# Transposing weight loads, a tanh gate and a new order of work in a fused attention and gate block

## The chip, the cores and the metric

The kernel runs on one core of a Trainium2 chip. The metric is device time in microseconds for one execution; lower is better. A core has five engines with instruction queues of their own: TensorE (PE, matrix products, with PEld for its weight loads), VectorE (DVE), ScalarE (ACT), GpSimd (POOL) and SyncE (SP), which here only issues DMAs. Sixteen DMA engines move the data.

## The reference

Two residual blocks over 2048 rows of 448 numbers in bf16. The first is linear attention with 16 heads of width 28 and learned feature maps, the second a gated layer with 1792 inner columns.

```python
x = A_x
h  = x + A(layernorm(x))
h2 = h + B(layernorm(h))

def A(x):                       # per head, width 28
    q, k, v = split(x @ wqkv)
    pq, pk = q @ w_phi[h], k @ w_phi[h]
    phi_q = concat(softmax(pq), softmax(-pq))
    phi_k = concat(softmax(pk), softmax(-pk))
    kv, z = phi_k.T @ v, phi_k.sum(rows)
    return (phi_q @ kv) / (phi_q @ z + 1e-6) @ wo   # heads side by side

def B(x):
    return (sigmoid(x @ w_gate) * (x @ w_up)) @ w_down
```

## The kernel before, in words

**Tiles.** The 2048 rows are 16 tiles of 128 rows (t = 0 to 15). The 448 columns are cut in four parts of 112 (KT) on the input side, in four groups of four heads (G) for features, and in seven parts of 64 (NJ) for the gated layer, where two products of 64 rows run side by side on TensorE. The gated layer works on chunks of 2, 4, 4, 4, 2 tiles (CH) with 14 blocks of 128 inner columns each.

**Fold.** `w_fold` (L547) multiplies the key weights, and then the query weights, by the feature weights ahead of time, so that one product gives pk or pq: wk and wq are loaded whole (L514, L517), transposed by TensorE in 32 small products (L555), evicted in eight copies (L562) to WkT and WqT, multiplied by a block-diagonal Wphi (L570) and evicted (L578) to Wk2 and Wq2.

**Key stage**, per tile: statistics (L590, L592, L593), the reciprocal root on GpSimd (L595), the normalised tile xn (L607 for tiles 0 and 1, else ScalarE at L612), its transpose xnT (TensorE and an eviction at L630 for the first NPE = 2 tiles, else one transposing DMA for two tiles, L633), the key product (kp, L648), two exponentials exp(pk) and exp(-pk) (L661, L663), their sums per head (ss, L672), reciprocals (rs, L675), the features phi = e/sum (L677, on GpSimd), the value product (vp, L656) with its eviction v1 (L669; by VectorE for tiles 3, 7, 11, 15, else ScalarE), and the product kv of features and values, gathered in two PSUM banks over all tiles (L686).

**Query products** (q, L704) come in groups g by chunks c of 512 rows: 16 groups, each followed by two exponentials eq (L715). Groups with c >= QLATE = 3 wait for the last key product.

**Ramp.** After the last kv: kvz (L722), per tile the numerators and denominators for both signs (num, L743), their eviction ocp (L749), a chain on VectorE (rSm, rr, b, c, rd, o; L760 to L774), the transpose oT (TensorE for tiles 0 and 1, else a transposing DMA, L794), the output projection wo_ (L801, L803), the residual sum h (L809), statistics (L812 to L817), hn and its transpose hT (L833 or L845).

**Gated layer**: per chunk and block, gate and up products (gu, L882 and L884), a sigmoid (sig, L891, ScalarE, to bf16), its product with up (hh, L899, VectorE), and per tile the down product (dn, L908; in halves for the last chunk, L918), the last sum (fin, L929) and the store (st, L932). Exponential and sigmoid are in different tables of ScalarE; `sigld` (L730) loads the sigmoid's table, after all eq, and every sigmoid waits for it. The first inner buffer hh0 lies on the memory of wqkv_sb, so the first hh wait for all query products and the last value product.

**Order.** `_Graph.task` takes each piece of work with its engine, an assumed duration and its dependences. `order` plays the program through with these durations: whenever an engine is free it takes the ready task that can start first, and among equals the one of the highest priority. The priorities are written out by hand in `PLACE` (a list of numbers for each kind of task; a lower number goes first). `emit` writes each engine's queue in that order, with semaphore waits; nothing is reordered on the chip. All DMAs but one go out from SP's one queue: x in six loads, the weights, the transposes, the stores. The late weights (wo, gate, up, down: `late`) wait for named xn tiles, wd for kvz. `trw` (L526) is a transpose of the identity whose result is not used. `plan_warm` puts products of the identity (L462) into TensorE's gaps.

Of the kernel before, what the change touches and what calls it, by code (L numbers as in the profile page):

```python
# [5 lines left out]
dt = mybir.dt  # L6
# [4 lines left out]
P = 128  # L11
D = 448
# [87 lines left out]
    "gu": """-149 -69 212 504 -67 499 571 613 553 686 662 556 704 811 760 897 430 682 831 777 916 981 800 922  # L100
        1060 933 899 1065 980 1044 1074 1055 1069 1091 1426 1071 1096 1414 1351 1802 1426 1463 1803 1796
        1792 1803 1804 1805 1841 1845 1857 1849 1914 1897 1891 1901 1973 1977 1913 1978 2489 2015 2513 2543
        2509 2613 2613 2544 2690 2667""",
    "sig": """948 372 885 604 191 749 554 125 566 -25 401 65 70 404 1365 1163 1121 1732 1149 1516 1414 1417 837
        1305 1745 568 1524 1733 1778 1672 1896 1696 2258 1698 1277 1813 1360 1866 1312 1490 1487 1911 1594
        2084 1373 1485 2455 1646 1813 1209 2197 1782 1347 2343 1785 1546 2315 2249 923 2294 1937 2190 2255
        1783 1989 1863 1460 2849 2249 2072""",
    "hh": """-350 -346 71 178 -275 119 344 313 177 836 837 195 770 762 1030 1300 355 1247 1023 1310 1073 1339
        1341 1165 1768 1355 1139 1150 1428 1144 1128 1619 1849 1209 1161 1615 1564 1460 1637 1568 1864 1791
        1386 1144 1440 1563 1682 1730 1603 1465 2178 1685 1693 1665 1679 1142 1889 2077 2002 1895 1899 2065  # L110
        1937 1755 2251 1517 1783 1620 1747 1911""",
# [15 lines left out]
class _Graph:  # L127
# [38 lines left out]
    def order(self):  # L166
# [55 lines left out]
        while True:  # L222
            best = None
            for e in self.ENGINES:
                cands = []
                for t in ready[e]:
                    est = max(free[e], port) if t.lock else free[e]
                    if e == "pe" and t.rows64 != rows64:
                        est += self.SWITCH
# [30 lines left out]
            elif t.kind == "tr":  # L260
                t.finish = max(t.finish, dma_free + 1.0)
# [720 lines left out]
```

## Time and profile before

| | us |
|---|---|
| median of 3 runs | 219.78 |
| lowest, highest | 219.76, 220.05 |
| profiled execution, its own time | 221.35 |
| span of that execution, first to last instruction | 219.6 |
| TensorE busy | 206.8 (94%) |
| VectorE busy | 133.4 (61%) |
| ScalarE busy | 116.5 (53%) |
| GpSimd busy | 52.5 (24%) |

Times in rows of the profile count from the start of the span. A matmul's busy time contains its way through the array, so that matmuls in a row overlap; what a run of them takes is read from the chain of waits, where "PE bank L648 x4" stands with the time until the next piece. L numbers are lines of the kernel before.

### The profile page before, as it was taken

The numbers are of one execution on the slowest core, as the hardware profiler recorded it, in microseconds if no ns is written. First come the engines' busy times: TensorE is split into PE (matmuls) and PEld (weight loads), VectorE is DVE, ScalarE is ACT, GpSimd is POOL, SyncE is SP. The second block draws the span as 40 slices with busy tenths as digits, with TensorE's granted clock in tenths as the row PEclk, the third lists the DMA queues.
The fourth block names the chain that finished last, engine by engine and source line by source line (L and its number), as shares of the span: only waits on it lengthen the run. The fifth ranks groups of instructions, "written<-read, shape, count | busy, mean of one in ns | idle before, by whom it ended". The sixth has DMA issues, their size and how long they took to land.

```text
span 219.6 us, 4860 instructions
## 1 busy us (share of the span) xinstructions
PE 206.8 (94%) x1912; PEld 119.3 (54%) x1912; DVE 133.4 (61%) x315; ACT 116.5 (53%) x203; POOL 52.5 (24%) x91
## 2 busy tenths in 40 slices
PE   6699997879999899999999999999999999999994
PEld 1665654546654577754444444445444455556893
DVE  2689878676299999996759754342344523224532
ACT  2689997975899748857554764220244321001420
POOL 5332898787101105072033300000000000000000
PEclk9889999999999999999999999999999999999999
DMA  6985999990282204566544740001000000111001
GB/s 173 277 165 94 199 179 201 198 154 3 63 226 48 43 3 72 98 128 149 109 41 84 87 84 1 3 8 56 23 0 3 0 3 32 51 42 44 1 3 42
DMA packets 37702, 17.51 MB, mean 80 GB/s; under 512 B 28912, under 2 KB 36784, under 8 KB 37680
## 3 DMA queue, kind: packets, MB, share of 16 engines
q1 hardware_dynamic: 37216, 17.19, 39.1%
q8 instruction: 15, 0.25, 0.4%
q10 hardware_dynamic: 464, 0.03, 0.1%
q14 instruction: 7, 0.06, 0.1%
HBM read 8.68 MB, written 1.84 MB: 48 GB/s over the span
## 4 chain that ended last, share of the span: by engine, by line
PE 67%; ACT 12%; DMA 10%; DVE 6%; issue 2%; SPq 1%; POOL 0%
PE bank L882 36%; PE bank L908 17%; DMA xnT<-xn_pad 6%; PE bank L801 4%; ACT eq L715 3%; DMA wqkv_sb<-in_A_wqkv_dram 3%; ACT xn_pad L612 2%; PE bank L918 2%; ACT ek L661 2%; PE bank L704 2%; ACT opm L749 2%; PE bank L656 2%; ACT v L669 1%; ACT ek L663 1%; DMA oT<-o_pad 1%
## 5 line engine op out<-in xcount | busy, mean ns | idle before, releaser
L882 PE MATMUL bank<-hnT,wgu_sb 64*128 64x512 bf16 (+1 forms) x490 | 87.2, 333 | 0.5 <-DVE st L812 0.3
L884 PE MATMUL bank<-hnT,wgu_sb 64*128 64x512 bf16 (+1 forms) x490 | 87.2, 334 | 0.0
L891 ACT ACTIVATE sg_sb<-bank 128x512 bf16<-128x512 f32 (+1 forms) x70 | 35.6, 510 | 74.8 <-PE bank L884 69.4
L882 PEld LDWEIGHTS bank<-hnT,wgu_sb 64*128 64x128 bf16 x490 | 45.4, 94 | 38.5 <-issue 1.2
L899 DVE TENSOR_TENSOR hh<-sg_sb,bank 128x512 bf16<-128x512 bf16 (+1 forms) x70 | 40.4, 579 | 40.3 <-ACT sg_sb L891 37.9
L884 PEld LDWEIGHTS bank<-hnT,wgu_sb 64*128 64x128 bf16 x490 | 45.3, 94 | 0.0
L908 PE MATMUL bank<-wd_sb,hh 128*128 128x448 bf16 x196 | 37.6, 353 | 0.2 <-DVE hh L899 0.2
L908 PEld LDWEIGHTS bank<-wd_sb,hh 128*128 128x128 bf16 x196 | 18.9, 98 | 18.7 <-issue 0.8
L677 POOL TENSOR_TENSOR phi<-ek,rsum 128x896 bf16<-128x896 bf16 x16 | 27.0, 1697 | 8.7 <-DVE rs L593 4.2
L929 DVE TENSOR_TENSOR x_sb<-bank,x_sb 128x448 bf16<-128x448 f32 (+1 forms) x18 | 10.2, 572 | 22.7 <-PE bank L908 19.0
L817 POOL TENSOR_TENSOR rs<-rs,neghalf 128x1 f32<-128x1 f32 x16 | 10.1, 634 | 53.0 <-DVE rs L815 52.9
L672 DVE TENSOR_REDUCE ssum<-ek 128x32 f32<-128x896 bf16 x16 | 17.1, 1070 | 7.4 <-ACT ek L663 5.9
L715 ACT ACTIVATE eq<-bank 112x512 bf16<-112x512 f32 x32 | 18.6, 647 | 1.9 <-PE bank L704 1.9
L841 ACT ACTIVATE hn_pad<-x_sb,nm,rs 128x896 bf16<-128x896 bf16 x14 | 15.8, 1129 | 3.6 <-POOL nm L839 2.3
L648 PE MATMUL bank<-Wk,xnT 112*128 112x448 bf16 x64 | 14.6, 353 | 3.3 <-DMA xnT<-xn_pad 3.3
L749 ACT CAST opm<-bank 128x960 bf16<-128x960 f32 x16 | 15.2, 968 | 2.9 <-PE bank L743 2.3
L704 PE MATMUL bank<-xnT,Wq 112*112 112x512 bf16 x64 | 16.4, 381 | 0.1
L656 PE MATMUL bank<-wqkv_sb,xnT 112*128 112x448 bf16 x64 | 15.1, 360 | 0.0
L590 DVE BATCH_NORM_STATS2 st<-x_sb 128x6 f32<-128x448 bf16 x16 | 9.7, 615 | 5.8 <-DMA x_sb<-in_A_x_dram 5.8
L801 PE MATMUL bank<-wo_sb,oT 64*128 64x448 bf16 x56 | 11.9, 349 | 0.4 <-DMA oT<-o_pad 0.3
L803 PE MATMUL bank<-wo_sb,oT 64*128 64x448 bf16 x56 | 11.9, 350 | 0.0
L612 ACT ACTIVATE xn_pad<-x_sb,nm,rs 128x448 bf16<-128x448 bf16 x14 | 10.4, 802 | 1.6 <-DMA xnT<-xn_pad 1.6
(80 smaller groups left out, 217.5 us busy)
## 6 DMA issues: line engine op xcount, KB each, us to landing
wgu_sb<-in_B_w_gate_dram SPq DMA_DIRECT2D x7, 224.0 KB, 6.0
wgu_sb<-in_B_w_up_dram SPq DMA_DIRECT2D x7, 224.0 KB, 5.8
wd_sb<-in_B_w_down_dram SPq DMA_DIRECT2D x7, 224.0 KB, 5.5
out_dram<-x_sb SPq DMA_DIRECT2D x14, 112.0 KB, 1.7
x_sb<-in_A_x_dram SPq DMA_DIRECT2D x3, 448.0 KB, 7.1
wqkv_sb<-in_A_wqkv_dram SPq DMA_DIRECT2D x3, 392.0 KB, 6.2
wo_sb<-in_A_wo_dram SPq DMA_DIRECT2D x8, 98.0 KB, 4.8
x_sb<-in_A_x_dram SPq DMA_DIRECT2D x1, 224.0 KB, 3.3
```

The source lines that it names most:

```text
L656: r = e.matmul(bank[b][:, 0:D], lhsT=xT(t, kt), rhs=wqkv_sb[:, kt, 2 * D:3 * D], start=(kt == 0), stop=(kt == KT - 1))
L672: task(("ss", t), "dve", 1.0, lambda e, s=s: e.tensor_reduce(ssum[:, s, :], ek[:, s, :, :].rearrange("p a (h d) -> p (a h) d", d=DH), AX.X ...
L677: task(("phi", t), "pool", 1.66, lambda e, t=t, s=s: e.tensor_tensor(phi[:, t % NPHI, :, :].rearrange("p a (h d) -> p (a h) d", d=DH), ek[ ...
L704: r = e.matmul(bank[b][:GP, :], lhsT=Wq2[:, kt, g * GP:(g + 1) * GP], rhs=xnT[:GP, 2 * c:2 * c + 2, :, kt, :], start=(kt == 0), stop=(kt = ...
L715: task((key, g, c), "act", 0.48, lambda e, g=g, c=c, sg=sg, nm=nm: e.activation(eq[c][:, sg, g, :], bank[got(nm)[0]][:GP, :], ACT.Exp, sca ...
L749: task(("ocp", t), "act", 0.845, lambda e, t=t: e.copy(opm[:, (t // 2) % 2, :, t % 2, :, :].rearrange("p b e h -> p b (e h)"), pair[got((" ...
L801: e.matmul(bank[b[0]][:, 0:D], lhsT=oT[0:64, tb, j, :], rhs=wo_sb[0:64, j, :], start=(j == 0), stop=(j == NJ - 1))
L882: e.matmul(bank[bg][:, 0:N], lhsT=wgu_sb[0:64, j, fs], rhs=hnT[0:64, j, cs], start=(j == 0), stop=(j == NJ - 1))
L884: r = e.matmul(bank[bu][:, 0:N], lhsT=wgu_sb[64:P, j, fs], rhs=hnT[64:P, j, cs], start=(j == 0), stop=(j == NJ - 1), tile_position=(64, 0))
L891: task(("sig", f_, c), "act", 0.487 if n == 4 else 0.27, lambda e, j=j, N=N, nm=nm: e.activation(sg_sb[:, j % NSG, 0:N], bank[got(nm)[0]][ ...
L899: task(("hh", f_, c), "dve", 0.605 if n == 4 else 0.34, lambda e, j=j, N=N, nm=nm, f_=f_, c=c: e.tensor_tensor(hhT[c % 2][:, f_, 0:N], sg_ ...
L908: r = e.matmul(bank[b][:, 0:D], lhsT=hhT[c % 2][:, f_, ts], rhs=wd_sb[:, f_, :], start=(f_ == 0), stop=(f_ == FT - 1))
```

## The change

- **Query and key weights.** wk and wq are not loaded. One transposing DMA each (`wT`, on SP) reads 512 columns of the weights from DRAM straight into WkT and WqT, in four blocks of 128 columns by 448. Blocks of 128 don't end where heads of 28 do, so Wphi gets two forms with blocks of six heads, zeros outside (masks maskW, two more products on GpSimd, four small loads from ScalarE's queue), and a fold takes up to two products per block. Only the value weights are loaded plainly (wv_sb). `trw` goes.
- **Gate.** sigmoid(g) = (tanh(g/2) + 1)/2: ScalarE writes tanh with scale 0.5 in f32, VectorE does (t + 1) * up in one operation, and the last sum multiplies by 0.5. `sigld` and the waits on it go; hh0 lies on wv_sb, Wk2, ek and phi, and the first hh wait for the last kv.
- **Late weights** wait for no tile; each gets a place in time in `PLACE`, before which `order` doesn't issue it.
- **Engines.** phi for tiles 5, 10 and 15 on VectorE; all v1 on ScalarE; tiles 2 and 3 transposed by TensorE too (NPE 4).
- **Query products** of chunks 1 to 3 wait for the last key product (QLATE 1), and the query fold uses banks 6 and 7 only.
- **Planner.** DMAs are assumed with other durations; all priorities in `PLACE` are new numbers.

```diff
-    "wk": """-54""",
-    "wq": """-31""",
-    "x": """-49 97 -66 153 194 403""",
-    "wv": """162""",
+    "x": """-1482 -1481 -1420 -108 80 110""",
+    "wv": """20""",
+    "wT": """-449 -50""",
-    "wo": """-284 -237 -109 -270 210 -133 380 376""",
-    "wg": """-425 -159 279 392 352 243 416""",
-    "wu": """-92 -32 -21 632 225 32 510""",
-    "wd": """306 59 205 -189 414 -101 56""",
+    "wo": """371 117 227 433 467 476 394 505""",
+    "wg": """505 491 155 372 315 471 206""",
+    "wu": """198 348 590 208 258 610 602""",
+    "wd": """385 721 711 677 665 660 781""",
...
+                    if t.kind == "in" and t.prio is not None:
+                        est = max(est, -0.1 * t.prio)
...
-            if t.kind == "in":
-                dma_free = max(dma_free, est + 1.5) + t.size / 300.0
-                t.finish = dma_free + 1.0
-            elif t.kind == "tr":
-                t.finish = max(t.finish, dma_free + 1.0)
+            if t.kind is not None:
+                dma_free = max(dma_free, est + 1.2) + t.size
+                t.finish = dma_free + t.full
...
-    NPE = 2
+    NPE = 4
-    QLATE = 3
+    QLATE = 1
-    V_DVE = (3, 7, 11, 15)
+    V_DVE = ()
+    PHI_DVE = (5, 10, 15)
...
-        sg_sb = sb("sg_sb", [P, NSG, 512])
+        sg_sb = sb("sg_sb", [P, NSG, 512], dt.float32)
...
+            task(("Wphi", w), "pool", 1.35, lambda e, w=w: e.tensor_tensor(
+                Wphi[:, w, :, :, :], Wphi0[:, w, :, None, :].to_broadcast([P, 4, 6, DH]),
+                maskW[:, w, :, :, None].to_broadcast([P, 4, 6, DH]), ALU.mult),
+                [("wphi", w, 0), ("wphi", w, 1), ("mphi0", w), ("mk2", w)])
...
-                    for kt in range(KT):
-                        r = e.transpose(bank16[b][:GP, kt * GP:(kt + 1) * GP],
-                                        wqkv_sb[:, kt, w * D + g * GP:w * D + (g + 1) * GP], ident[:GP, :GP])
+            WT, W2, c0, h0 = (WqT, Wq2, 0, 0) if w == 0 else (WkT, Wk2, D - 64, -2)
+            task(("wT", w), "sp", 1.3, lambda e: e.dma_start_transpose(out=WT[:, :, :], in_=A_wqkv[:, c0:c0 + 512]),
+                 lat=-0.4, size=2.1, kind="tr")
...
-                    for g in range(G):
-                        r = e.matmul(bank[b][:GP, g * GP:(g + 1) * GP], lhsT=WT[:, g, kt * GP:(kt + 1) * GP],
-                                     rhs=Wphi[:, g, :], start=True, stop=True)
+                    old = 0
+                    for k in range(4):
+                        base = 4 * k + h0
+                        hi = min(base + 6, H)
+                        for lo, z in ((max(base, 0), old), (old, hi)):
+                            if lo < z:
+                                r = e.matmul(bank[b][:GP, lo * DH:z * DH], lhsT=WT[:, k, kt * GP:(kt + 1) * GP],
+                                             rhs=Wphi[:, w, k, lo - base:z - base, :], start=(k == 0), stop=(k == 3 and z == hi))
+                        old = hi
...
-            task(("phi", t), "pool", 1.66, lambda e, t=t, s=s: e.tensor_tensor(
+            task(("phi", t), "dve" if t in PHI_DVE else "pool", 1.0 if t in PHI_DVE else 1.66, lambda e, t=t, s=s: e.tensor_tensor(
...
-        task("sigld", "act", 1.4, lambda e: e.activation(junk[:, 0:1], neghalf[:, 0:1], ACT.Sigmoid),
-             EQ_ALL + ["neghalf"])
...
-                    sg_sb[:, j % NSG, 0:N], bank[got(nm)[0]][:, 0:N], ACT.Sigmoid),
+                    sg_sb[:, j % NSG, 0:N], bank[got(nm)[0]][:, 0:N], ACT.Tanh, scale=0.5),
...
-                    hhT[c % 2][:, f_, 0:N], sg_sb[:, j % NSG, 0:N], bank[got(nm)[1]][:, 0:N], ALU.mult), deps, bias=bias)
+                    hhT[c % 2][:, f_, 0:N], sg_sb[:, j % NSG, 0:N], 1.0, bank[got(nm)[1]][:, 0:N], op0=ALU.add, op1=ALU.mult),
...
-                        xo, bank[got(nm)[0]][:, 0:w], xo, ALU.add),
+                        xo, bank[got(nm)[0]][:, 0:w], 0.5, xo, op0=ALU.mult, op1=ALU.add),
```

In the lists of late weights the numbers are tenths of a microsecond of the planner's time; in the list of x the first four loads go as soon as SP is free, by rank.

More of the change, by code (lines that the diff above doesn't have):

```diff
@@ L413, in build @@
         xnT = sb("xnT", [P, NT // 2, 2, KT, P])
-        wqkv_sb = sb("wqkv_sb", [GP, KT, 3 * D])
         Wq2 = sb("Wq2", [GP, KT, D])
-        Wk2 = sb("Wk2", [GP, KT, D])
-        Wphi0 = sb("Wphi0", [GP, G, DH])
-        Wphi = sb("Wphi", [GP, G, GP])
+        Wphi0 = sb("Wphi0", [P, 2, 4, DH])
+        maskW = sb("maskW", [P, 2, 4, 6])
+        Wphi = sb("Wphi", [P, 2, 4, 6, DH])
         wo_sb = sb("wo_sb", [P, NJ, D])
@@ L521, in build @@
         load_x(12, 16, bias=BIG - 8, dur=1.0)
-        load("wphi", Wphi0[:], A_w_phi.rearrange("(g hl) i j -> (hl i) g j", hl=HL), 25, bias=BIG, eng="act")
-        task("Wphi", "pool", 1.0, lambda e: e.tensor_tensor(
-            Wphi[:].rearrange("p g (h d) -> p g h d", h=HL), Wphi0[:][:, :, None, :].to_broadcast([GP, G, HL, DH]),
-            maskK[:][:, None, :, None].to_broadcast([GP, G, HL, DH]), ALU.mult), ["wphi", "maskK"])
-        task("trw", "sp", 1.25, lambda e: e.dma_start_transpose(out=oT[:, 0, 0, :], in_=ident[:]), ["ident"],
-             lat=2.8, kind="tr")
+        phi_rows = A_w_phi.rearrange("h i j -> (h i) j")
+        for w in range(2):
+            c0, one, z = (-64, slice(64, P), slice(0, 64)) if w else (0, slice(0, 64), slice(64, P))
+            full, part = (slice(1, 4), 0) if w else (slice(0, 3), 3)
+            task(("mphi0", w), "dve", 0.08, lambda e, w=w, z=z, part=part: e.memset(Wphi0[z, w, part, :], 0.0))
+            r0 = 64 if w else 0
+            load(("wphi", w, 0), Wphi0[:, w, full, :], phi_rows[r0:r0 + 384].rearrange("(b p) j -> p b j", p=P), 0.15,
+                 bias=BIG + w, eng="act")
+            r1 = 0 if w else 384
+            load(("wphi", w, 1), Wphi0[one, w, part, :], phi_rows[r1:r1 + 64], 0.1, bias=BIG + w, eng="act")
+            off = 8 if w else 0
+            task(("mk0", w), "pool", 0.15, lambda e, w=w: e.memset(maskW[:, w, :, :], 1.0))
+            task(("mk1", w), "pool", 0.2, lambda e, w=w, off=off: e.affine_select(
+                out=maskW[:, w, :, :], in_=maskW[:, w, :, :], compare_op=ALU.is_ge, fill=0.0, base=-off,
+                channel_multiplier=1, pattern=[[16, 4], [-DH, 6]]), [("mk0", w)])
+            task(("mk2", w), "pool", 0.2, lambda e, w=w, off=off: e.affine_select(
+                out=maskW[:, w, :, :], in_=maskW[:, w, :, :], compare_op=ALU.is_ge, fill=0.0, base=DH - 1 + off,
+                channel_multiplier=-1, pattern=[[-16, 4], [DH, 6]]), [("mk1", w)])
+            task(("Wphi", w), "pool", 1.35, lambda e, w=w: e.tensor_tensor(
+                Wphi[:, w, :, :, :], Wphi0[:, w, :, None, :].to_broadcast([P, 4, 6, DH]),
+                maskW[:, w, :, :, None].to_broadcast([P, 4, 6, DH]), ALU.mult),
+                [("wphi", w, 0), ("wphi", w, 1), ("mphi0", w), ("mk2", w)])
         late = []
@@ L655, in f @@
                 for kt in range(KT):
-                    r = e.matmul(bank[b][:, 0:D], lhsT=xT(t, kt), rhs=wqkv_sb[:, kt, 2 * D:3 * D],
+                    r = e.matmul(bank[b][:, 0:D], lhsT=xT(t, kt), rhs=wv_sb[:, kt, :],
                                  start=(kt == 0), stop=(kt == KT - 1))
@@ L692, in build @@
                  banks=[((4, 5), None)] if t == 0 else None, until=[("kvz", 0), ("kvz", 1)])
-        for name, dst, src, kb, dur, deps in late:
-            load(name, dst, src, kb, deps=deps, dur=dur)
+        for name, dst, src, took, dur, place in late:
+            load(name, dst, src, took, dur=dur, lat=0.65)
+            K.tasks[name].prio = -10 * place
         for c in range(NCH):
@@ L716, in build @@
                         eq[c][:, sg, g, :], bank[got(nm)[0]][:GP, :], ACT.Exp, scale=1.0 if sg == 0 else -1.0), [nm])
-        EQ_ALL = [(k, g, c) for k in ("eqp", "eqm") for g in range(G) for c in range(NCH)]
-        Q_ALL = [("q", g, c) for g in range(G) for c in range(NCH)]
         for sg in range(2):
```

121 lines of the change are left out of this document (55 added, 66 removed), and 130 rows, old and new, of the table PLACE.

## The prediction

> **What bounds the kernel now.** I read the page's span, slices and chain shares first, then the busy time by stretches, and then the chain of waits piece by piece.
>
> ```profile
> span 219.6 us, 4860 instructions
> PE   6699997879999899999999999999999999999994
> DMA  6985999990282204566544740001000000111001
> PE bank L882 36%; PE bank L908 17%; DMA xnT<-xn_pad 6%; PE bank L801 4%; ACT eq L715 3%; DMA wqkv_sb<-in_A_wqkv_dram 3%; ACT xn_pad L612 2%; PE bank L918 2%; ACT ek L661 2%; PE bank L704 2%; ACT opm L749 2%; PE bank L656 2%; ACT v L669 1%; ACT ek L663 1%; DMA oT<-o_pad 1%
> ```
>
> TensorE carries the end, but 10% of the chain is DMA: the loads of the query and key weights and the transposes of the normalised input. By stretches (span, PE, PEld, DVE, ACT, POOL busy, clock, DMA share, GB/s):
>
> ```profile
> 4.00:57.40 53.40, 48.00 (x372) 29.94 (x370) 40.64 (x95) 42.82 (x86) 34.79 (x33) 0.97 0.84 160
> 31.20:50.00 18.80, 15.51 (x127) 9.62 (x126) 13.43 (x20) 14.99 (x33) 15.23 (x12) 1.00 1.09 173
> 57.40:75.60 18.20, 16.42 (x173) 9.85 (x171) 15.84 (x48) 16.60 (x27) 1.49 (x2) 1.00 0.45 115
> 75.60:95.00 19.40, 18.80 (x282) 14.24 (x283) 18.84 (x55) 13.42 (x23) 4.43 (x12) 1.00 0.34 61
> 95.00:215.00 120.00, 120.00 (x1073) 63.31 (x1072) 56.63 (x117) 42.34 (x69) 9.72 (x30) 1.00 0.21 42
> ```
>
> From 95 to 215 us TensorE never rests, while VectorE and ScalarE work less than half the time. So the end can move only if TensorE gets its earlier work done sooner. That earlier work has two parts: the **key stage** (to the last feature product, L686) and the **ramp** (from there to about 95). Three engines are over 70% busy in 31 to 50 and the DMA engines are full (1.09). The chain of waits shows the ends of the parts:
>
> ```profile
> 2.40 6.20 DMA wqkv_sb<-in_A_wqkv_dram
> 9.46 0.53 PE bank L570 x8
> 14.54 0.54 ACT ek L663
> 31.24 6.89 DMA xnT<-xn_pad
> 42.19 6.79 DMA xnT<-xn_pad
> 49.03 0.93 PE bank L648 x4
> 50.38 0.76 PE bank L648 x4
> 56.40 0.42 PE bank L686 x8
> 56.81 0.88 PE bank L704 x4
> 75.63 0.27 PE bank L882
> ```
>
> The first key exponential is at 14.5, the key stage ends at 56.8, the first gate product is at 75.6. Two transposes (31.2 and 42.2) lie on the chain for 6.9 and 6.8 us. Against them stand the medians from issue to landing, and what SP had issued just before the second one:
>
> ```profile
> wqkv_sb<-in_A_wqkv_dram SPq DMA_DIRECT2D x3, 392.0 KB, 6.2
> x_sb<-in_A_x_dram SPq DMA_DIRECT2D x1, 224.0 KB, 3.3
> hnT<-hn_pad SPq DMA_TRANSPOSE x14, 2.9
> xnT<-xn_pad SPq DMA_TRANSPOSE x7, 6.3
> oT<-ident SPq DMA_TRANSPOSE x1, 7.9
> ```
> ```profile
> 0.79 0.46 SPq L503 DMA_DIRECT2D x_sb<-in_A_x_dram  x1
> 39.45 1.52 SPq L503 DMA_DIRECT2D wgu_sb<-in_B_w_gate_dram  x2
> 41.02 0.60 SPq L503 DMA_DIRECT2D wgu_sb<-in_B_w_up_dram  x1
> 42.19 1.23 SPq L633 DMA_TRANSPOSE xnT<-xn_pad  x1
> ```
>
> In a quiet queue a transpose lands in 2.9 us; behind three 224 KB loads it takes 6.8, so the late weights cost about 4 us at each of these two places.
>
> **The change part by part.**
>
> *Start.* The weights wk and wq no longer come as plain loads followed by 32 TensorE transposes and eight evictions (L555, L562); two transposing loads write WkT and WqT. In the new order SP issues x 0, x 1, x 2-3, WkT, so the WkT issue begins near 0.79 + 3 x 0.5 = 2.3. No row shows a transpose that reads DRAM. Its landing lies between 2.9 us (quiet) and 7.9 (oT<-ident, in the full queue of the start). I take 5.0, nearer the first end, since only 448 KB are queued ahead of it: 7.3. Four folds (L570, 0.53 us for eight matmuls, two folds in the old form; three eighths more columns in the new one) and an eviction of 0.6 (L578, quoted below) bring about 9.4, one key product (0.93 with its drain) 10.3, against 14.5: 4.2 us earlier, bounds 1.3 and 6.3. Value weights now come after both transposing loads, near 13, as late as before; no exponential waits for them, and the value product of a tile is wanted only with its features.
>
> The Trainium skill ("DMA: Bandwidth & Descriptors", Why small descriptors are slow) speaks against this part: DRAM reads in 256-byte pieces lose about 3 cycles in 11. The same page (Latency and other measured facts) gives a transpose 261 GB/s, by which, as an estimate, 459 KB take 1.8 us; no run here shows either. By these figures WkT lands nearer 6 than 7.3 and the sum improves by about 1 us.
>
> *Key stage.* VectorE gets three feature products (896 elements each), loses four value evictions and the four W copies; GpSimd loses three products; ScalarE gets the four value evictions and two more input evictions.
>
> ```profile
> L677 POOL TENSOR_TENSOR phi<-ek,rsum 128x896 bf16<-128x896 bf16 x16 | 27.0, 1697 | 8.7 <-DVE rs L593 4.2
> L672 DVE TENSOR_REDUCE ssum<-ek 128x32 f32<-128x896 bf16 x16 | 17.1, 1070 | 7.4 <-ACT ek L663 5.9
> L669 DVE CAST v<-bank 128x448 bf16<-128x448 f32 x4 | 2.4, 609 | 0.6 <-PE bank L656 0.4 <-PE bank L686 0.2
> L562 DVE COPY WqT<-bank 112x448 bf16<-112x448 bf16 x2 | 0.8, 377 | 0.0
> L578 DVE CAST Wk<-bank 112x448 bf16<-112x448 f32 x2 | 1.2, 602 | 0.0
> L590 DVE BATCH_NORM_STATS2 st<-x_sb 128x6 f32<-128x448 bf16 x16 | 9.7, 615 | 5.8 <-DMA x_sb<-in_A_x_dram 5.8
> ```
>
> A feature product on VectorE is not in the trace: between 1.07 (the sum over the same 896 elements) and 1.70 (on GpSimd); I take 1.07, since it is the same engine and length. VectorE then has 40.6 + 3 x 1.07 - 2.4 - 1.5 = 39.9 us from 4.1 on. GpSimd has 34.8 - 5.1 = 29.7 plus about 3 for the second Wphi and its masks. ScalarE loses twelve exponentials (next part), about 6.3, and gains six evictions of at most 0.6: 40.1 or less, and part of that overlaps. So VectorE paces the stage, with ScalarE close behind. Never idle, it ends at 44, and the last kv near 45; idle 12.8 us as now, at 56.8. Of the present idle time 5.8 is the wait for x (L590), which stays, and 7.4 the wait of L672 on the exponentials, mostly behind the late transposes, which goes where their queue is clear. I take 6 us idle: 50.0, and 50.3 with the last kv. **Term 1: -6.5**, bounds 0 and -11.8.
>
> *Query products.* With QLATE 1 the products of chunks 1 to 3 wait for the last key product.
>
> ```profile
> L704 PE MATMUL bank<-xnT,Wq 112*112 112x512 bf16 x26 | 6.8, 381 | 0.1
> L884 PE MATMUL bank<-hnT,wgu_sb 64*128 64x256 bf16 x98 | 12.0, 270 | 0.0
> L743 PE MATMUL bank<-kvz,eq 112*128 112x120 bf16 x120 | 8.7, 217 | 0.9 <-ACT opm L749 0.9
> L801 PE MATMUL bank<-wo_sb,oT 64*128 64x448 bf16 x35 | 7.4, 350 | 0.4 <-DMA oT<-o_pad 0.3
> 63.10 2.11 ACT L715 ACTIVATE eq<-bank 112x512 bf16<-112x512 f32 x4
> ```
>
> These are counts in 57.4 to 95. Some 26 matmuls (six groups of four) of the query product run there now; after it will be twelve, so six groups of 0.86 us (5.2 on TensorE) and twelve exponentials of 0.53 (6.3 on ScalarE) move behind the last key product. That product ends some 5 us ahead of the last kv (the key product at 50.4 to 51.1 against 56.8), and there TensorE has room: two groups fit, 1.7 us. **Term 2: +3.5**, bounds +1.7 and +5.2.
>
> *Ramp.* TensorE's own work in 57.4 to 95, by spacings: query 6.5 x 0.87 = 5.6; numerators 15 x 0.42 = 6.3; output projection 5 x 7 x 0.19 = 6.7; gate and up 98 x 0.109 = 10.7 (256 against 448 columns at 0.19); small transposes about 2: 31 of 37.6 us, a **gap** of 6. The added query work can lie in it, as nothing in the gate chain of tiles 0 to 5 waits for chunks 2 and 3, and no sigmoid waits for all exponentials. Against it, ScalarE is busy 16.6 of 18.2 at the ramp's front, where a table load goes:
>
> ```profile
> L730 ACT ACT_TABLE_LOAD x1 | 1.3, 1283 | 0.0
> ```
>
> I take half the gap. **Term 3: -3.0**, bounds 0 and -6.
> The weights for the down projection now go out between oT and hT transposes instead of in one run at 58; behind a load these land up to 4 us later (6.9 against 2.9), but the same query work covers TensorE there: nothing, with 4 us if it isn't there. The gate and up weights lose their waits on xn and stand at written places up to 61 us in SP's one queue, each behind the transposes ahead of it; issued by 61 and landed within 6.2 (the 392 KB row) they are there at 67, ahead of a first gate product that comes 18.8 us after the last kv (75.6 less 56.8), at 69. Later places would cost their whole lateness.
>
> *Gate.* tanh with scale 0.5 into f32, (t + 1) times u in one VectorE operation, the half in the last sum: as many instructions, elements and PSUM operands as before. Behind 120 us of unbroken TensorE they cost nothing; doubled, VectorE's 56.6 us would still fit. Only the five last gates of a chunk and the last sum are bare: 0, bounds -0.5 and +1.
>
> **Sum**: -6.5 + 3.5 - 3.0 = -6.0 on the span of 219.6, thus 213.6. The profiled execution took 221.35, 1.75 more than its span; the median of the runs, 219.78, lies 0.2 above the span, so the forecast for the runs is **213.8**.
>
> **The rivals.**
> 1. *The stage packs.* Transposes land in 3 us throughout, VectorE idles 3 us less, and two thirds of the gap fill: -9.5 + 3.5 - 4 = -10: 209.8. For it: the 7.4 us of waits on exponentials. Against: four engines with 30 to 40 us each leave little slack.
> 2. *The queue wins.* The start's DMA is full (slices at 8 to 9), and the transposing loads put off x 8-15 and wv; keys begin 1.3 earlier only. Stage -3: -3 + 3.5 - 3 = -2.5: 217.3.
> 3. *Slower: the query products lose their cover.* If VectorE idles as it does now, the stage ends near 55.3 (-1.5) with TensorE idle where six query groups lay; all 5.2 come behind it, and ScalarE, full at the ramp's front, holds up the numerators, so that only 1 us of the gap fills: -1.5 + 5.2 - 1 = +2.7: 222.5. It decides when the stage ends later than 56.8 - 4.2 = 52.6.
> 4. *Not one table.* If tanh and exp took turns in the tables, each turn costs 1.28; eight turns in the ramp, 10 us on an engine with 1.6 spare there: about +2 over all, 222. The trace shows a single load for exp, identity and copy together, and none for tanh. The Trainium skill ("ScalarE: Activation LUTs", Table sets) puts exp and tanh in one set; by that this rival falls.
>
> **How the numbers follow.** Forecast 0.50, packed stage 0.16, queue 0.14, lost cover 0.14, tables 0.03; 0.03 falls between the last three, within 0.2% of before (0.44 us, about what these runs can tell from no change). So faster 0.80, same 0.03, slower 0.17. The range reaches from below the packed stage to just over no change, 208.0 to 220.5, and leaves out the slower cases; the forecast's own range is 211 to 217.
>
> **What would show it.** First ek near 10.3 (before 14.5); last L686 near 50 (56.8); xnT landings with a median near 3 to 4 (6.3); VectorE busy 38 to 41 to the stage's end; query products after the last key product, TensorE without gaps over 1 us from 60 on; one table load; 95 to the end unchanged in length per product. A WkT landing after 10, a last kv after 52.6, or loads between exp and tanh would prove it wrong.

## The result, and the profile after

The changed kernel takes 214.73 us (median of 4 runs, 213.96 to 214.87) against 219.8 for the kernel before (median of 4, 219.76 to 220.05). The ratio is 0.976, 95% interval 0.9735 to 0.9784: 5.1 us faster, where 6.0 was forecast and 213.8 named. Line numbers below are those of the changed kernel, where L578 is the fold, L629 the transpose of a normalised tile on TensorE, L656 is the key product, L664 the value product, L694 the product kv, L685 the features, L713 the query product, L807 the output projection, L890 and L892 gate and up, L915 the down product.

The page of the changed kernel, the lines that answer to those shown of before:

```profile
span 212.9 us, 4844 instructions
PE   6799999999998998999999999999999999999994
DMA  6975773991037357564315610001000001111001
PE bank L890 38%; PE bank L915 18%; PE bank L807 4%; PE bank L713 4%; PE bank L656 3%; PE bank L664 3%; ACT eq L724 3%; DMA WkT<-in_A_wqkv_dram 2%; PE bank L925 2%; DMA oT<-o_pad 2%; ACT xn_pad L620 2%; PE bank L694 2%; ACT opm L753 2%; PE bank L578 1%; PE bank L747 1%
```

The input transposes are gone from the chain, DMA's share falls from 10% to 4%, and TensorE's slices are at 8 or 9 tenths from the third one on until the last. By stretches (columns as before), cut at the new ends of the parts:

```profile
4.00:49.80 45.80, 44.40 (x366) 27.98 (x365) 38.92 (x88) 41.22 (x85) 31.41 (x32) 1.00 0.81 175
49.80:68.60 18.80, 17.85 (x180) 11.11 (x178) 15.75 (x46) 17.09 (x29) 1.50 (x2) 1.00 0.30 64
68.60:95.00 26.40, 25.27 (x327) 17.50 (x329) 24.30 (x73) 16.47 (x27) 7.68 (x23) 1.00 0.57 127
```

The chain of waits shows where the parts end now, and one new wait:

```profile
2.18 5.13 DMA WkT<-in_A_wqkv_dram
7.36 0.93 PE bank L578 x14
8.29 0.23 PE bank L629 x4
8.51 0.37 PE bank L578 x7
8.91 1.22 DVE Wk L586 x2
10.27 0.92 PE bank L656 x4
48.96 0.84 PE bank L694 x16
68.73 0.27 PE bank L890
80.39 4.39 DMA oT<-o_pad
88.02 5.47 PE bank L915 x28
```

The key weights land at 7.3. The first exponential (11.22 in the timeline) comes 3.3 us earlier than in before's profile, the key stage ends at 49.8 instead of 56.8, the first gate product comes at 68.7 instead of 75.6, and the first down product at 88.0 instead of 94.6. So the whole gain is there at the end of the key stage: 3.3 us of it come before the first exponential, 3.7 between there and the last kv (38.6 us for 42.3). The ramp (last kv to first down product) takes 38.2 us, before 37.8. Two kinds of transposes and the transposing load of the key weights, median from issue to landing:

```profile
hnT<-hn_pad SPq DMA_TRANSPOSE x14, 2.6
xnT<-xn_pad SPq DMA_TRANSPOSE x6, 3.1
WkT<-in_A_wqkv_dram SPq DMA_TRANSPOSE x1, 5.1
```

The input transposes took 6.3 before. VectorE's wait for x, 5.8 before, has shrunk too:

```profile
L598 DVE BATCH_NORM_STATS2 st<-x_sb 128x6 f32<-128x448 bf16 x16 | 9.4, 611 | 2.7 <-DMA x_sb<-in_A_x_dram 2.7
```

The gate operations keep their durations, 595 ns for ScalarE and 685 for VectorE, against the 595 and 686 ns of before in the view by line and shape:

```profile
L905 DVE SCALAR_TENSOR_TENSOR hh<-sg_sb,bank 128x512 bf16<-128x512 f32 x42 | 28.6, 685 | 31.5 <-ACT sg_sb L899 31.3
L899 ACT ACTIVATE sg_sb<-bank 128x512 f32<-128x512 f32 x42 | 24.8, 595 | 43.7 <-PE bank L892 41.3 <-DVE hh L905 1.5 <-DVE mv L820 0.9
```

**Two different gains.** The spans of the two profiles differ by 6.7 us, the medians of the runs by 5.1. Both profiled executions end some 1.75 us after their spans (221.35 on 219.6; 214.7 on 212.9), so the median run of before has a span of about 218.0: before's profiled execution was 1.6 us longer than its median run. The four runs of before beside the result lie close together, but in the three jobs of the experiments its medians were 220.6, 221.0 and 221.2, near the profiled execution. `gate_sigmoid` below, whose median is that of the changed kernel (214.7), was 6.0 us faster than before in its own job. So the 5.1 holds for the four runs of the result, and the kernel before varies by more than the difference between 5.1 and 6.7. Its stretches at the start show one thing that varies (last three columns: the clock that TensorE was granted, as a share of the full one, DMA share, GB/s):

```profile
5.00:10.00 5.00, 2.94 (x39) 2.43 (x39) 3.14 (x15) 2.60 (x5) 1.46 (x3) 0.96 1.09 279
10.00:15.00 5.00, 4.95 (x39) 3.57 (x39) 5.00 (x17) 4.07 (x10) 1.14 (x2) 0.70 1.13 235
```

TensorE was busy 2.94 of 5 us while it waited for weights, and from 9.6 to 13.0 ran at half clock (0.70 over 5 us is 3 us at half), just when fold and first products were due. The Trainium skill ("TensorE: Matmul & The Clock Gate", Part 1) has the clock halve after an idle window of about 3.4 us. This trace shows no such window: between its first product and 9.6 TensorE's longest pause was 1.66 us (6.98 to 8.64), and in the 3.4 us ahead of 9.6 it was busy for 1.75.

### The profile page after: what moved, and what is told of

It is laid out like the page before. It is cut to its first block, busy times and chain, and to the rows that moved or that the text cites. A ratio compares the mean times of both kernels' runs of the same rounds, so it can differ in the third digit from the quotient of the medians.

```text
span 212.9 us, 4844 instructions
## 1 busy us (share of the span) xinstructions
PE 204.5 (96%) x1914; PEld 118.3 (56%) x1914; DVE 133.9 (63%) x312; ACT 114.4 (54%) x203; POOL 48.7 (23%) x95
## 4 chain that ended last, share of the span: by engine, by line
PE 79%; ACT 10%; DMA 4%; DVE 3%; issue 2%; SPq 1%
PE bank L890 38%; PE bank L915 18%; PE bank L807 4%; PE bank L713 4%; PE bank L656 3%; PE bank L664 3%; ACT eq L724 3%; DMA WkT<-in_A_wqkv_dram 2%; PE bank L925 2%; DMA oT<-o_pad 2%; ACT xn_pad L620 2%; PE bank L694 2%; ACT opm L753 2%; PE bank L578 1%; PE bank L747 1%
## 5 line engine op out<-in xcount | busy, mean ns | idle before, releaser
L890 PE MATMUL bank<-hnT,wgu_sb 64*128 64x512 bf16 (+1 forms) x490 | 87.2, 333 | 0.3 <-DVE x_sb L815 0.3
L892 PE MATMUL bank<-hnT,wgu_sb 64*128 64x512 bf16 (+1 forms) x490 | 87.2, 333 | 0.0
L899 ACT ACTIVATE sg_sb<-bank 128x512 f32<-128x512 f32 (+1 forms) x70 | 35.5, 510 | 76.0 <-PE bank L892 71.3
L890 PEld LDWEIGHTS bank<-hnT,wgu_sb 64*128 64x128 bf16 x490 | 45.4, 94 | 38.2 <-issue 1.2
L905 DVE SCALAR_TENSOR_TENSOR hh<-sg_sb,bank 128x512 bf16<-128x512 f32 (+1 forms) x70 | 40.2, 578 | 36.9 <-ACT sg_sb L899 36.7
L892 PEld LDWEIGHTS bank<-hnT,wgu_sb 64*128 64x128 bf16 x490 | 45.3, 94 | 0.0
L915 PE MATMUL bank<-wd_sb,hh 128*128 128x448 bf16 x196 | 37.6, 353 | 0.2 <-DVE hh L905 0.2
L915 PEld LDWEIGHTS bank<-wd_sb,hh 128*128 128x128 bf16 x196 | 18.9, 98 | 18.7 <-issue 0.8
L936 DVE SCALAR_TENSOR_TENSOR x_sb<-bank,x_sb 128x448 bf16<-128x448 f32 (+1 forms) x18 | 10.3, 571 | 24.8 <-PE bank L915 21.2
L685 POOL TENSOR_TENSOR phi<-ek,rsum 128x896 bf16<-128x896 bf16 x13 | 21.8, 1698 | 4.2 <-DVE rsum L683 4.1
L713 PE MATMUL bank<-xnT,Wq 112*112 112x512 bf16 x64 | 15.9, 380 | 0.4 <-ACT eq L724 0.4
L656 PE MATMUL bank<-Wk,xnT 112*128 112x448 bf16 x64 | 14.6, 352 | 0.7 <-DVE Wk L586 0.6
L664 PE MATMUL bank<-wv_sb,xnT 112*128 112x448 bf16 x64 | 14.7, 352 | 0.0
L807 PE MATMUL bank<-wo_sb,oT 64*128 64x448 bf16 x56 | 11.9, 349 | 0.9 <-DMA oT<-o_pad 0.8
L713 PEld LDWEIGHTS bank<-xnT,Wq 112*112 112x112 bf16 x64 | 7.7, 130 | 4.7 <-ACT eq L724 0.7
```

What stands on the lines that cost most here:

```text
L656: r = e.matmul(bank[b][:, 0:D], lhsT=xT(t, kt), rhs=Wk2[:, kt, :], start=(kt == 0), stop=(kt == KT - 1))
L664: r = e.matmul(bank[b][:, 0:D], lhsT=xT(t, kt), rhs=wv_sb[:, kt, :], start=(kt == 0), stop=(kt == KT - 1))
L685: task(("phi", t), "dve" if t in PHI_DVE else "pool", 1.0 if t in PHI_DVE else 1.66, lambda e, t=t, s=s: e.tensor_tensor(phi[:, t % NPHI, ...
L713: r = e.matmul(bank[b][:GP, :], lhsT=Wq2[:, kt, g * GP:(g + 1) * GP], rhs=xnT[:GP, 2 * c:2 * c + 2, :, kt, :], start=(kt == 0), stop=(kt = ...
L807: e.matmul(bank[b[0]][:, 0:D], lhsT=oT[0:64, tb, j, :], rhs=wo_sb[0:64, j, :], start=(j == 0), stop=(j == NJ - 1))
L890: e.matmul(bank[bg][:, 0:N], lhsT=wgu_sb[0:64, j, fs], rhs=hnT[0:64, j, cs], start=(j == 0), stop=(j == NJ - 1))
```

## The experiments

Since the kernel before ran between 219.6 and 223.3 us in the jobs of the experiments, more widely than with the result, I compare an experiment with the changed kernel (214.7, profiled span 212.9) by its median, its span and the times of its parts, and give the ratio to before in the same job with its 95% interval. The changed kernel itself was not run again in these jobs.

**1. What paces the key stage: four runs that take work from one engine or move it to another.** The forecast's theory is VectorE; the rivals are TensorE, ScalarE, or no engine alone.

`phi_gpsimd`, features of tiles 5, 10, 15 back on GpSimd:

```diff
         done = self.order()
+        for t in done:
+            if t.name in (("phi", 5), ("phi", 10), ("phi", 15)):
+                t.eng = "pool"
```

> The changed kernel with the feature products of tiles 5, 10 and 15 back on GpSimd, each at the same place in the order. VectorE loses some 3.5 us, GpSimd gains 5.1 (31.4 to 36.5 of 45.8 us). The forecast's theory, VectorE paces the key stage: the last kv ends 2 to 3 us before 49.8 and the time falls to 212 to 213. Rival, TensorE paces it (4.8 of every 5 us in products from 10 us on): the last kv stays within 0.7 of 49.8, later by the longer last product at most, 214.5 to 215.5. Third: GpSimd becomes the pace, last kv 52 or later, 216.5 or more.

Measured: median 216.17 (214.69 to 217.49), ratio 0.9802 (0.9725 to 0.988); span 212.9, last kv at 50.5. Two of its four runs had a granted clock of 0.992 and spans of 215.7 and 215.8; the two at full clock have 212.9 and 213.1 and took 214.7 and 214.9. Its stretch of the key stage:

```profile
7.00:49.80 42.80, 41.68 (x349) 26.46 (x349) 33.93 (x76) 40.68 (x84) 34.39 (x33) 1.00 0.78 169
```

In the changed kernel the same stretch has VectorE 37.17 and GpSimd 29.67. VectorE lost 3.2 us, GpSimd gained 4.7, and the stage ended 0.7 us later, not 2 to 3 earlier. So the forecast's theory fails this test, but the test is not clean: GpSimd's last four products stand one behind the other from 43.2 to 49.9, and so GpSimd, not VectorE, ends this run's stage. The changed kernel's own chain says more: from the first exponential to the last kv VectorE stands on it for 1.5 us only (29.9 to 31.3). At full clock the three products on VectorE bring nothing to the end.

`half_value`, TensorE relieved (half of each value sum left out):

```diff
-                for kt in range(KT):
+                for kt in range(2):
                     r = e.matmul(bank[b][:, 0:D], lhsT=xT(t, kt), rhs=wv_sb[:, kt, :],
-                                 start=(kt == 0), stop=(kt == KT - 1))
+                                 start=(kt == 0), stop=(kt == 1))
```

> The changed kernel with two of the four products that make up each tile's values left out (the values are then sums over half the columns); order and all else kept. TensorE has 32 x 0.19 = 6.1 us less in the key stage. TensorE paces the stage: the last kv ends 4 to 6 us earlier (44 to 46) and the time falls to 209 to 211. VectorE or ScalarE paces it: last kv at 48.5 or later, and the time falls by at most 2, to 212.7 or more.

Measured: median 213.23 (213.08 to 213.71), ratio 0.9675 (0.9621 to 0.973), span 211.5, last kv at 49.25. 6.1 us of TensorE work less end the stage 0.55 us earlier: the rival that I held likely after the result falls too. (The time falls by 1.5; the other 0.9 arises between the first gate product and the first down product, 18.3 us for 19.3, where this run left out nothing, and its cause is not shown.) Its chain of waits in the last part of the stage:

```profile
37.16 1.10 DVE ssum L680
39.53 1.08 DVE phi L685
41.38 1.24 issue
42.62 1.71 POOL phi L685
44.41 0.54 ACT ek L671
44.95 0.45 ACT ek L669
45.42 1.10 DVE ssum L680
46.54 0.36 DVE rsum L683
46.93 1.66 DVE phi L685
```

Here exponential, sum, reciprocal and feature product follow each other from engine to engine. In the chain of the changed kernel itself TensorE stands without a break from 37.6 to 49.8:

```profile
37.63 0.92 PE bank L656 x4
48.96 0.84 PE bank L694 x16
```

So TensorE does end the stage there, but another chain follows half a microsecond behind it, and relieving TensorE only uncovers it.

`narrow_values`, ScalarE relieved (half of each value eviction left out):

```diff
...
-                dst = v1[:, t % NV, :, 0:DH]
+                dst = v1[:, t % NV, :, 0:14]
...
```

> The changed kernel with each value eviction on ScalarE cut to the first 14 of a head's 28 columns (the other half of the values is left at one); order and instruction counts kept. ScalarE has 16 x 0.19 = 3.0 us less in the key stage. ScalarE paces the stage: last kv 2 to 3 us before 49.8, time 212 to 213. No engine alone paces it (VectorE and TensorE relieved brought 0 and 0.6): last kv within 0.8 of 49.8, time 213.9 to 214.9.

Measured: median 214.64 (214.36 to 215.35), ratio 0.9713 (0.9657 to 0.9769), span 212.6, last kv at 50.3, with a first exponential 0.8 later than in the changed kernel (12.0), as the key weights landed after 5.9 us instead of 5.1; so the stage itself is 0.3 us shorter. ScalarE alone does not pace it. With ScalarE relieved, TensorE is busy in all of the 38.27 us from first exponential to last kv (columns as before), and the chain of waits there holds nothing but its products.

```profile
12.00:50.27 38.27, 38.27 (x317) 24.82 (x315) 33.87 (x71) 35.32 (x78) 26.70 (x25) 1.00 0.79 158
```

`v_vector`, value evictions of tiles 3, 7, 11, 15 back on VectorE:

```diff
...
-            def f(e, t=t, eng="dve" if t in V_DVE else "act"):
+            def f(e, t=t, eng="dve" if t in (3, 7, 11, 15) else "act"):
```

> The changed kernel with the value evictions of tiles 3, 7, 11 and 15 back on VectorE at the same places in the order: VectorE +2.4 us, ScalarE -2.4. VectorE paces the stage: last kv near 52, time 216.5 to 217. TensorE paces it: last kv within 0.7 of 49.8, time 214.3 to 215.3. ScalarE paces it (41.2 of 45.8 us busy): last kv near 48, 213.

Measured: median 215.17 (214.93 to 217.34), ratio 0.978 (0.9715 to 0.9846), span 213.2, last kv at 50.85. It comes 1.05 later, where VectorE as the pace gave 2 and ScalarE as the pace -2: between the theories, and it decides nothing alone.

What follows: the stage has two limits about half a microsecond apart. The work of TensorE fills 38.3 us of the 38.6, as `narrow_values` shows, so it cannot get much shorter without less of it. With TensorE relieved of 6.1 us, the chain through ScalarE, VectorE and GpSimd holds it at 38.1. So relieving one engine alone shortens the stage by about half a microsecond at most. That the second limit is the loop of exponential, sum, feature product and kv over three ek and two phi buffers is argued from the rows of `half_value`, not shown; no run relieves both.

**2. The late weights.** `late_as_before` puts them back to their old places in SP's queue:

```diff
         done = self.order()
...
+        ahead = {4: wo[0:2], 6: wg[0:1], 8: wo[2:4] + wg[1:2] + wu[0:3] + wg[2:3] + wo[4:5], 10: wo[5:8],
+                 12: wg[3:4] + wu[3:5] + wg[4:5], 14: wu[5:6] + wg[5:7] + wu[6:7]}
...
+            if t.name[0] == "xT" and t.name[1] in ahead:
+                rest += [ld[n] for n in ahead[t.name[1]]]
...
```

> The changed kernel with the late loads at the places in SP's queue that they had before (the same loads ahead of each input transpose, all of down behind the last), all other queues in the same order. The forecast's step: each of the late transposes lands about 4 us later, the last kv 4 to 8 us later, time 218 to 221. Rival: the stage has slack for it, since tiles are normalised well ahead: last kv less than 1.5 us later, time below 216.2.

Measured: median 219.42 (218.65 to 221.32), ratio 0.9926 (0.9888 to 0.9965), span 217.9, last kv at 55.5. The transposes' median is 5.0 us, and two are on the chain again:

```profile
26.41 6.14 DMA xnT<-xn_pad
41.65 5.88 DMA xnT<-xn_pad
```

The stage ends 5.7 us later, 0.75 of it from a later first exponential (12.0), so 4.9 within the stage. Part of this is the clock: TensorE paused for 2.5 us (30.1 to 32.6) for the first of the two transposes, its clock was halved from 33.9 to 37.3, and the fastest run, at full clock, has a span of 216.8, 1.1 less than the profiled one. Against the changed kernel's 214.7 this one edit gives back 4.7 us; against before in the same job (221.0) 1.6 us of gain, 0.7%, are left. Either way it is most of what the change gained. The stage of 43.5 us from first exponential to last kv is then no shorter than before's 42.3, so the rest of the change does not visibly shorten the stage once the start is taken off.

`before_loads_behind` makes the edit from the other side, in the kernel before:

```diff
         done = self.order()
...
+        k = [t.name for t in sp].index(("xT", 10))
+        z = [t.name for t in sp].index(("xT", 14))
+        move = [t for t in sp[k:z] if t.kind == "in"]
+        rest = [t for t in done if t not in move]
+        i = rest.index(sp[z]) + 1
+        done = rest[:i] + move + rest[i:]
```

> The kernel before with the eight gate and up loads that stand ahead of the last two input transposes moved behind the last of them; nothing else changed. The forecast's step: these transposes land in about 3 us instead of 6.8, and the time falls by 3 to 6, to 214 to 217 on before's 219.8. Rival: the exponentials and the TensorE work set the pace anyway, and under 1.5 us comes back: 218.3 or more.

Measured: median 219.6 (218.41 to 222.77), ratio 0.9933 (0.9894 to 0.9972), span 217.0, last kv at 53.2. The rival holds: 1.4 us by the medians of the same job (219.6 against 221.0). My choice covered one of the two places only, since the wait at 31.2 is the transpose xT 10 itself, behind loads that I left; it stays on the chain:

```profile
29.40 7.49 DMA xnT<-xn_pad
36.93 0.93 PE bank L655 x4
```

The wait at 42.2 is gone, and the stage from first exponential to last kv is 40.55 us instead of 42.3: one such place is worth 1.8 us in the stage, not 4. From the first gate product to the first down product this run then takes 19.9 us, where before takes 18.95 and its repeat below 19.5, so up to 1.0 is lost again.

**3. The start.** `before_again` is the kernel before, unchanged, in search of a start at full clock.

> The kernel before, unchanged, once more, for a profile in which the clock is full all the way. In the profile that the forecast was made from, the granted clock was 0.70 between 10 and 15 us. If that dip made the late first exponential (14.5), this profile has it near 12.7, as the run with the loads behind had, the last kv near 55, and a span of 218.0 to 218.5 instead of 219.6; the start then gains 1.4 us and not 4.2. If the dip lay beside waits, the first exponential stays near 14.5.

Measured: one run, 222.78, span 221.1, and not what was expected: first exponential at 15.3. The page gives it a mean clock of 1.0, but its trace has no entry of the clock before 14.6, and its products are slow until then, first this run and then before's first profile, from their chains of waits:

```profile
8.40 1.37 PE bank L555 x12
15.33 0.55 ACT ek L663
```
```profile
8.64 0.82 PE bank L555 x12
```

Twelve transposes took 1.37 us at 8.4 where they took 0.82. So this start was cold. In `before_loads_behind`, whose queues are those of before up to the moved loads, the clock was full from 5.0 on and the first exponential came at 12.7. But the clock is not all of the difference. The second load of weights, for which these twelve transposes wait, is issued at 2.40 in all three profiles and landed after 6.2, 6.0 and 5.2 us:

```profile
2.40 6.20 DMA wqkv_sb<-in_A_wqkv_dram
2.39 5.97 DMA wqkv_sb<-in_A_wqkv_dram
2.40 5.20 DMA wqkv_sb<-in_A_wqkv_dram
```

(Before, `before_again`, `before_loads_behind`.) Of the 1.9 us between 14.5 and 12.7, 1.0 is there when the load lands, before the clock is halved, and 0.9 follows, most of it while it is. The kernel before thus has its first exponential anywhere from 12.7 to 15.3, by the landing of this load and by the clock.

`wk_after_wq` lets the query weights go first:

```diff
         done = self.order()
+        a = [t.name for t in done].index(("wT", 1))
+        b = [t.name for t in done].index(("wT", 0))
+        done[a], done[b] = done[b], done[a]
```

> The changed kernel with the two transposing weight loads in the other order, so that the key weights land about 3 to 4 us later and the first exponential comes at 14 to 15 instead of 11.2; nothing else changed. The forecast's step takes the start whole into the stage's end: last kv 2.5 to 4 us later, time 217 to 218.5. Rival, the stage makes up for it, as its work is bound elsewhere: last kv under 1.5 later, time below 216.2.

Measured: median 220.72 (218.86 to 221.41), ratio 0.9967 (0.9936 to 0.9998), span 219.2, first exponential 17.0, last kv 56.8. The weights land 3.5 us later (10.8 for 7.3), but TensorE, waiting for them, then worked at half clock from 10 to 20 us:

```profile
10.00:20.00 10.00, 8.80 (x62) 6.49 (x63) 5.39 (x16) 5.47 (x11) 1.80 (x4) 0.51 0.47 143
```

5.8 us at the first exponential become 7.0 at the last kv and 6.3 at the end. So a delay of the start does go whole into the end. Here the late weight cost nearly twice its lateness; the 2.3 us between 3.5 and 5.8 arose while TensorE ran at half clock.

`plain_weights`, the old fold in the changed kernel:

```diff
...
-            WT, W2, c0, h0 = (WqT, Wq2, 0, 0) if w == 0 else (WkT, Wk2, D - 64, -2)
-            task(("wT", w), "sp", 1.3, lambda e: e.dma_start_transpose(out=WT[:, :, :], in_=A_wqkv[:, c0:c0 + 512]),
+            WT, W2, key, src_w = (WqT, Wq2, "wq", wq_sb) if w == 0 else (WkT, Wk2, "wk", wk_sb)
...
+                        r = e.transpose(bank16[b][:GP, kt * GP:(kt + 1) * GP],
+                                        src_w[:, kt, g * GP:(g + 1) * GP], ident[:GP, :GP])
...
```

> The changed kernel with the old fold: key and query weights loaded plainly at the places in SP's queue of the transposing loads, 32 TensorE transposes, eight evictions, one block-diagonal Wphi; the order of all queues is planned anew with the changed kernel's priorities. The forecast's step: first key exponential 3 us later than 11.2 (14 to 14.5) and the time 2.5 to 4 us longer, 217.2 to 218.7. Rival: plain loads in a queue without the others ahead come sooner than in the kernel before and the later stage takes up the rest: first exponential near 12.5, time 215.5 or less.

Measured: median 228.85 (228.79 to 229.36), ratio 1.0346 (1.0282 to 1.041). The first exponential comes at 13.9, 2.7 later, but the order planned anew with priorities made for another kernel lets the first down product slip to 118.7 (88.0). The time is that of the new order, not of the fold: for the time it decides nothing, and what the transposing loads alone are worth at the end stays open.

**4. The ramp and the gate.** `half_query` leaves out half of each query sum of chunks 2 and 3:

```diff
-                    for kt in range(KT):
+                    n = KT if c < 2 else 2
+                    for kt in range(n):
...
```

> The changed kernel with two of the four products left out in each query group of chunks 2 and 3 (sums over half the columns); order kept. TensorE has 8 x 0.43 = 3.4 us less between 45 and 64. The forecast's step, the added query work lies in a gap of the ramp: the first gate product stays within 0.6 of 68.7 and the time within 0.7 of 214.7. Rival, it takes TensorE's time from the gate chain: first gate product 2 to 3.4 us earlier, time 211.5 to 212.7.

Measured: median 214.48 (214.13 to 215.31), ratio 0.9702 (0.9653 to 0.975), span 212.6, first gate product at 68.5 (68.7). 3.4 us of TensorE work less change nothing beyond 0.3: the query work does lie in a gap.

`gate_sigmoid`, every queue in the same order:

```diff
-                    sg_sb[:, j % NSG, 0:N], bank[got(nm)[0]][:, 0:N], ACT.Tanh, scale=0.5),
+                    sg_sb[:, j % NSG, 0:N], bank[got(nm)[0]][:, 0:N], ACT.Sigmoid, scale=1.0),
...
```

> The changed kernel with every queue in the same order, but the gate as sigmoid(g) times up, and the last sum without the half. ScalarE gets one table load of 1.28 us in the ramp, after the last query exponential (66.4) and ahead of the first gate (about 70); the gate operations keep their sizes. If ScalarE holds the ramp (17.1 of 18.8 us busy between the last kv and the first gate product), the first hh and all behind it come 1.0 to 1.3 us later: 215.7 to 216.0 against 214.7. If VectorE's chain or the transposes hold the ramp, the load lies in ScalarE's idle time: 214.5 to 215.0.

Measured: median 214.67 (214.44 to 215.35), ratio 0.9741 (0.9693 to 0.9789), span 212.7. The load is there (69.4 us, 1.28) and costs nothing: ScalarE does not hold the ramp at this place, and the tanh as such gains no time.

`late_early` moves the nine late loads of the ramp ahead of its first transpose:

```diff
         done = self.order()
...
+        k = [t.name for t in sp].index(("oT", 2))
+        move = [t for t in sp[k:] if t.kind == "in"]
+        rest = [t for t in done if t not in move]
+        i = rest.index(sp[k])
+        done = rest[:i] + move + rest[i:]
```

> The changed kernel with the nine late weight loads that SP issues between the oT and hT transposes of the ramp (three of up, six of down) moved ahead of the first of these, to about 45 us, where the DMA engines are idle until 60. If these loads hold up the transposes on the chain (oT issued at 80.4 lands after 4.4 us, median 2.7), the TensorE gap at 80 to 85 (1.6 us) shrinks and the time falls by 0.7 to 1.5, to 213.2 to 214.0. If the gap comes from two transposes behind each other or from VectorE, nothing changes: 214.4 to 215.0.

Measured: median 214.14 (213.66 to 214.53), ratio 0.9683 (0.9611 to 0.9754), span 211.9. The stretch from 80 to 88 us, the changed kernel first, then this one:

```profile
80.00:88.00 8.00, 7.03 (x105) 4.68 (x99) 6.89 (x25) 6.08 (x11) 4.02 (x12) 1.00 0.68 129
```
```profile
80.00:88.00 8.00, 7.81 (x109) 5.26 (x106) 7.87 (x27) 7.06 (x12) 4.04 (x12) 1.00 0.48 101
```

TensorE's pause there shrinks by 0.8, the transpose is off the chain, and the first down product comes 1.0 earlier. The span is 1.0 shorter than the changed kernel's and the median 0.6. This does not show that the loads made the pause. `phi_gpsimd`, `v_vector`, `half_value` and `narrow_values` left them in place and take 18.3 to 18.5 us from the first gate product to the first down product, as this run does with 18.3, where the changed kernel takes 19.3. And the runs overlap (213.7 to 214.5 against 214.0 to 214.9).

## Why the prediction was right or wrong, point by point

- **Start.** WkT landed after 5.1 us (I took 5.0), so at 7.3 as forecast and not nearer 6, where the estimate of 1.8 us for its transfer would have put it. The first exponential came at 11.2, not 10.3, since two input transposes stood between the folds on TensorE (8.29 in the chain is one of them) and the last two evictions of Wk followed each other on VectorE (8.91 to 10.1), where I had counted one. Against the profile the gain is 3.3 instead of 4.2. The 14.5 in that profile came from a late load and from half clock; against the 12.7 of `before_loads_behind` the gain is 1.5. I had the granted clock of that stretch before me, quoted a row with 0.97 and passed over it. And the sum has no term for the start: term 1 counts VectorE's work from 4.1 on. `wk_after_wq` shows that a shift of the start goes whole into the end.
- **Key stage, -6.5.** Measured -7.0 between the profiles, 3.3 of it from the start. The size held, the mechanism did not: VectorE does not pace the stage. In the new stage TensorE's own work (38.3 of 38.6 us) and a chain through the other engines are limits of almost the same length. VectorE was busy 38.9 us and idle 6.9 where I took 39.9 and 6, but the idle time fell in another way: the wait for x, which I said stays at 5.8, fell to 2.7. That the term fits is in part luck. The step on the late weights was right in kind, and `late_as_before` shows it as the main cause. "About 4 us at each of these two places" was too large: one place measured 1.8 in the kernel before, both together 4.9 in the changed kernel, half clock included. That they cost more there because the stage has less other work to hide them is a guess.
- **Query products, +3.5, and ramp, -3.0.** Together they stand in the sum with +0.5; measured, the ramp grew by 0.4 (37.8 to 38.2). 29 of the 64 query matmuls began before the last kv ended, seven groups, where I had counted six; `half_query` shows that the later ones lie in a gap. I took the down weights between the ramp's transposes at nothing; `late_early` brings 1.0 at the first down product, but that they cost this is not shown, since runs that left them in place gain as much there.
- **Gate, 0.** Right: same durations, no second table, and with the table load back no difference either.
- **Sum and scale.** -6.0 against -6.7 by the profiles and -5.1 by the runs. The step that failed is "the median of the runs lies 0.2 above the span": it sets the median of some runs against the span of another execution, while a run lies 1.75 above its own span. The four runs of the result were 1.6 us shorter than the one I read; the later jobs, with 220.6 to 221.2, were much nearer to it. That the named 213.8 lies 0.9 from the measured 214.7 is therefore in part luck: a start without a term, a wrong pace and a wrong scale partly cancelled.
- **Rivals.** The queue (217.3), the lost cover (222.5) and the tables (222) did not come. The packed stage (209.8) did not either: its transposes did land in 3.1 us, but VectorE idled 6.9 us and not 3.

## What to carry to other kernels

Place late loads behind a transpose in the queue, not ahead of it: a wait of 3 us became 5 to 7 behind them here, and this one edit was worth most of the change. Where four engines are each over two thirds busy in a stage, relieve them one by one before naming the bound, and expect that relieving one uncovers the next. Before setting a sum against a profile, compare its time with many runs, from more than one job, and look at the clock of the stretch that the sum is about.

## What the runs showed of the hardware that was not expected

The clock at the start differs between executions of the same order of work: three profiles of the kernel before, one of them with later loads moved, had it full from 5.0 us, halved from 9.6 to 13.0, or cold until 14.6, with the first exponential at 12.7, 14.5 and 15.3. What decides it is not shown. The clock was also halved without a long pause: between its first product and 9.6 TensorE had paused for 1.66 us at most, and in `late_as_before` a single pause of 2.5 us was followed by 3.4 us at half clock, so that a late transpose can cost more than its wait. The mean granted clock of a run does not show a cold start (1.0 for the last of the three), the duration of the same few matmuls does (0.82 and 1.37 us). The same load at the same place in the queue landed up to 1.0 us apart: the second weight load of before after 5.2 to 6.2 us, the transposing load of the key weights (459 KB from DRAM) after 4.9 to 5.9 where it went first. A feature product of 896 elements took 1.09 us on VectorE in the median and 1.70 on GpSimd.
